# The head of an FFT filter and snake MLP kernel: PSUM as one block with rings, fewer and larger blocks of classes, products per filter part

## The chip, the cores and the metric

The kernel runs on one core of one Trainium2 chip. Its engines are TensorE (PE, with weight loads as PEld), VectorE (DVE), ScalarE (ACT), GpSimd (POOL) and SyncE (SP, which issues DMAs). Each engine works through its own queue in order and waits on semaphores for the others. The time is device microseconds of one execution.

## The reference

x has 8 batches of 3008 rows and 256 channels. Each batch is filtered in the frequency domain along its rows, and the 24,064 rows that result go through a two-layer network with the snake function.

```python
X = np.fft.rfft(x, axis=1)
Y = X * (filt_r + 1j * filt_i)[None]
x = np.fft.irfft(Y, n=3008, axis=1).reshape(24064, 256)
h = x @ w_in                                   # 256 -> 2048
g = h + np.sin(alpha * h) ** 2 / (alpha + 1e-9)
return g @ w_out                               # 2048 -> 256
```

## The kernel before, in words

**The transform.** 3008 is 47 x 64. A batch goes through a first small DFT over 47 (matmuls "pa"), a second one over 64 for each of 24 classes of frequencies ("pb", evicted as xf), products with the filter, the inverse of the second ("pc", evicted as g) and the inverse of the first ("pd", evicted as y). The filter lies in filt_t as two parts: f_t[0] holds filt_r and f_t[1] filt_i with signs, each on 128 partitions of which one half is loaded and the other is made on the chip by `other_half` (lines 439 to 446): a copy of 64x3072 elements for part 0, a negated one for part 1, each for two groups of 12 classes.

**The head** (lines 448 to 586) does batch 0 by itself, since nothing else can run yet. Turns of 32x32 blocks on VectorE (`turn`, line 473) take the place of trips through memory: four before the forward step, two large ones (`turn_back`) behind the inverse one. In between stand 12 blocks of 4 classes and 128 columns each (`blocks`, line 484). For each, `forward_0` has 4 matmuls and an eviction by ScalarE (line 495), `product_0` one VectorE product of 1024 elements that reads the block twice by a broadcast, once for each filter part (line 501), and `inverse_0` 8 matmuls (line 513) and an eviction, by ScalarE for all blocks (lines 516, 185). The loop of line 554 issues product i, inverse i-1, forward i+6, and in steps 5 and 6 the two halves of the filter's second group. `inverse_table` (line 420) makes a second table from the first through PSUM. `warm_pe` runs matmuls on zeros whose result nobody reads. Behind the last product GpSimd scales the weights w_in (line 542) and loads x of batch 1 in between (line 168).

**The main loop** (lines 746 to 760) has 48 chunks of rows. Eight steps a chunk each do two `hidden` (two ph matmuls, line 601; the sine on ScalarE as cos_all, line 605; v on VectorE, line 606) and some `project` (po matmuls, line 621, evicted as o at line 630 and stored). The transforms of batches 1 to 7 are placed into the steps by times written out by hand (`put` and `slot`): `first` and `first_tiled` (pa), `forward` (pb, xf), `product` and `cross` (the fused product of later batches), `inverse` (pc) and `last` (pd). `forward` evicts xf on ScalarE and sends its halves crosswise to xs by two DMAs on SP (line 250); `product` (line 257) reads xf, `cross` (lines 263, 264) reads xs.

**What sets the order around the change.** PSUM's eight banks are three pools: fps with two banks for all transform matmuls, hps with four for ph, warm-ups and the head's forward blocks, ops with two for po, the tables and the reciprocals. The SBUF pools xfpool (3 buffers), xspool (3) and ppool (7) hold xf, xs and the products. Whoever takes a buffer waits for the readers of its last tenant. Evictions by `evac` (line 182) without a given engine go to VectorE every third time and otherwise to ScalarE.

Of the kernel before, what the change touches and what calls it, by code (L numbers as in the profile page):

```python
# [9 lines left out]
FP16 = mybir.dt.float16  # L10
# [12 lines left out]
NR = 2 * N1  # L23
# [48 lines left out]
def kernel(  # L72
# [38 lines left out]
    xfpool = pool("xf", 3)  # L111
    ppool = pool("pp", 7)
    xspool = pool("xs", 3)
# [4 lines left out]
    fps = pool("fps", 2, PSUM)  # L118
    hps = pool("hps", 4, PSUM)
    ops = pool("ops", 2, PSUM)  # L120
# [31 lines left out]
    f_t = [filt_t[:, k] for k in range(2)]  # L152

# [35 lines left out]
    class Spectral:  # L189
# [13 lines left out]
        def first(self, i):  # L203
            ch, j = divmod(i, 4)
            ps = fps.tile([128, 512], FP32, name=f"pa_{self.b}_{i}", tag="f")
            marks["pe"] = nc.tensor.matmul(out=ps[0:NK, :], lhsT=wf_t, rhs=self.x[ch][:, 2 * j:2 * j + 2, :],  # L206
                                           start=True, stop=True)
            r0 = 8 * (ch % 2)
            evac(t1_h[ch // 2][0:NK, r0 + 2 * j:r0 + 2 * j + 2, :], ps[0:NK, :])
            if j == 3:  # L210
                nc.sync.dma_start(out=self.d1_rows[:, 8 * ch:8 * ch + 8, :], 
                                  in_=t1_h[ch // 2][0:NK, r0:r0 + 8, :])

        def first_tiled(self, ch):
            r0 = 8 * (ch % 2)
            for q in range(2):
                own, tag = (hps, "h") if q else (fps, "f")
                ps = [own.tile([128, 512], FP32, name=f"pa_{self.b}_{ch}_{q}_{h}", tag=tag) for h in range(2)]
                for h in range(2):
                    for c in range(2):  # L220
                        n = 4 * c + 2 * q
                        nc.tensor.matmul(out=ps[h][64 * c:64 * c + 64, :], lhsT=wt_t[64 * h:64 * h + N1],  # L222
                                         rhs=self.x[ch][64 * h:64 * h + N1, n:n + 2, :], start=True, stop=True)
                for h in range(2):
                    evac(t1_h[ch // 2][:, r0 + 4 * h + 2 * q:r0 + 4 * h + 2 * q + 2, :], ps[h], h == 0)
            d1 = self.d1.rearrange("a (h n) c -> a h (n c)", h=2)
            for c in range(2):
                n0 = (8 * ch + 4 * c) * C
                nc.sync.dma_start(out=d1[:, :, n0:n0 + 4 * C],
                                  in_=t1_h[ch // 2][64 * c:64 * c + 2 * NS, r0:r0 + 8, :]  # L230
                                  .rearrange("a (h n) c -> a h (n c)", h=2))
# [6 lines left out]
        def forward(self, u):  # L238
            b = self.b
            ps = fps.tile([128, 2, C], FP32, name=f"pb_{b}_{u}", tag="f")  # L240
            for i in range(2):
                s = 2 * u + i
                nc.tensor.matmul(out=ps[:, i, :], lhsT=d_t[:, s, :],  # L243
                                 rhs=self.t2[s // 6][:, s % 6, :], start=True, stop=True)
            self.xf[u] = xfpool.tile([128, 2, C], FP16, name=f"xf_{b}_{u}", tag="xf")
            nc.scalar.copy(out=self.xf[u], in_=ps)  # L246
            if self.fused:
                self.xs[u] = xspool.tile([128, 2, C], FP16, name=f"xs_{b}_{u}", tag="xs")
                for p in range(2):
                    nc.sync.dma_start(out=self.xs[u][64 * p:64 * p + 64, :, :],  # L250
                                      in_=self.xf[u][64 - 64 * p:128 - 64 * p, :, :])

        def product(self, u):
            self.p[u] = []
            for k in range(1 if self.fused else 2):
                pt = ppool.tile([128, 2, C], FP16, name=f"p_{self.b}_{u}_{k}", tag="p")
                marks["prod", u] = nc.vector.tensor_tensor(out=pt, in0=self.xf[u],  # L257
                                                           in1=f_t[k][:, 2 * u:2 * u + 2, :], op=ALU.mult)
                self.p[u].append(pt)
# [6 lines left out]
        def inverse(self, w):  # L266
# [4 lines left out]
            ps = fps.tile([128, 2, C], FP32, name=f"pc_{b}_{w}", tag="f")  # L271
# [12 lines left out]
        def inverse_tiled(self, w):  # L284
            g = gpool.tile([128, 4, 2, C], FP16, name=f"gt_{self.b}_{w}", tag="g")
            for q in range(2):
                own, tag = (hps, "h") if q else (fps, "f")
                ps = [own.tile([128, 2, C], FP32, name=f"pc_{self.b}_{w}_{q}_{k}", tag=tag) for k in range(2)]
# [20 lines left out]
        def last(self, u):  # L309
            ch, rest = divmod(u, 4)  # L310
            half, cb = divmod(rest, 2)
            n0 = 8 * ch + 4 * half
            ps = fps.tile([128, 4, 128], FP32, name=f"pd_{self.b}_{u}", tag="f")
            psv = ps.rearrange("p a b -> p (a b)")[:, 0:4 * NR].rearrange("p (a r) -> p a r", r=NR)
            for i in range(4):
                nc.tensor.matmul(out=psv[:, i, :], rhs=wi_t if self.b < TILED else wh_t, start=True, stop=True,  # L316
                                 lhsT=t4_h[ch // 2][0:NK, n0 % 16 + i, cb * 128:cb * 128 + 128])
            evac(y[:, cb, self.b % 2, n0:n0 + 4, :], psv)
# [29 lines left out]
    def spread_alpha(i):  # L348

        ps = hps.tile([128, 4, 128], FP32, name=f"al_bc_{i}", tag="h")  # L350
# [42 lines left out]
    def last_0(n0, n, own=fps, tag="f", spread=False):  # L393

        for cb in range(2):
            made = []

            def one(i, cb=cb, made=made):

                if i == 0:  # L400
                    ps = own.tile([128, 512], FP32, name=f"pd_0_{n0}_{cb}", tag=tag)
                    made.append(ps[:, 0:n * NR].rearrange("p (a r) -> p a r", r=NR))
# [11 lines left out]
    def reciprocals():  # L414

        ps = ops.tile([128, 512], FP32, name="ps_rec", tag="o")
# [3 lines left out]
    def inverse_table(g):  # L420

        gs = slice(8 * g, 8 * g + 8)
        ps = ops.tile([128, 8, 128], FP16, name=f"pse_{g}", tag="o")
# [6 lines left out]
    warmed = []  # L430

    def warm_pe(n):

        warmed.append(n)
        ps = hps.tile([128, 512], FP32, name=f"warm_{len(warmed)}", tag="h")
# [3 lines left out]
    def other_half(g, k, on_act):  # L439

        gs = slice(12 * g, 12 * g + 12)
        if k == 0:
            evac(f_t[0][64:128, gs, :], f_t[0][0:64, gs, :], on_act)
# [12 lines left out]
    for i in range(16):  # L456
        own, tag = (fps, "f") if i % 3 == 2 else (hps, "h")
        ps = own.tile([128, 512], FP32, name=f"pa_0_{i}", tag=tag)
# [21 lines left out]
    for i in range(4):  # L480
        turn(t2_0[i // 2][:, :, 32 * (i % 2):32 * (i % 2) + 32], t1_0[:, :, 32 * i:32 * i + 32])
        if i > 1:
            other_half(0, i - 2, False)
    blocks = [(hc, w) for hc in range(2) for w in range(3)] + [(0, 3), (1, 3), (0, 4), (0, 5), (1, 4), (1, 5)]
    xf0, p0 = {}, {}

    def forward_0(i):
        hc, w = blocks[i]
        ps = hps.tile([128, 4, 128], FP32, name=f"pb_0_{i}", tag="h")
        for j in range(4):  # L490
            nc.tensor.matmul(out=ps[:, j, :], lhsT=d_t[:, 4 * w + j, :],  # L491
                             rhs=t2_0[hc][:, 4 * w + j], start=True, stop=True)
        own, tag = (xspool, "xs") if i % 2 else (xfpool, "xf")
        xf0[i] = own.tile([128, 4, 128], FP16, name=f"xf_0_{i}", tag=tag)
# [3 lines left out]
    def product_0(i):  # L498
        hc, w = blocks[i]
        p0[i] = xpool.tile([128, 2, 4, 128], FP16, name=f"p_0_{i}", tag="x")  # L500
        marks["products"] = nc.vector.tensor_tensor(
            out=p0[i].rearrange("p f s (k c) -> p f s k c", k=2),
            in0=xf0[i].rearrange("p s (k c) -> p s k c", k=2)[:, None].to_broadcast([128, 2, 4, 2, 64]),
            in1=filt_t[:, :, 4 * w:4 * w + 4].rearrange("p f s (k c) -> p f s k c", k=2)[..., 64 * hc:64 * hc + 64],
            op=ALU.mult)

    def inverse_0(i):
        hc, w = blocks[i]
        ps = fps.tile([128, 4, 128], FP32, name=f"pc_0_{i}", tag="f")
        for j in range(4):  # L510
            s = 4 * w + j
            for k in range(2):
                nc.tensor.matmul(out=ps[:, j, :], rhs=p0[i][:, k, j, :],  # L513
                                 lhsT=e_t[:, s, :] if k == 0 else e1_0[:, s, :],
                                 start=(k == 0), stop=(k == 1))
        evac(g_0[hc][:, 4 * w:4 * w + 4], ps.rearrange("p s (k c) -> p s c k", k=2), not (i in ()))
# [31 lines left out]
    [inverse_table(g) for g in range(2)]  # L548
    for i in range(6):
        forward_0(i)  # L550
        if i % 3 == 2:
            if i == 2: inverse_table(2)
            warm_pe((4, 0)[i // 3])
    for i in range(13):
        for e in {5: [(1,0,False)],6: [(1,1,False)]}.get(i, ()):
            other_half(*e)
        if i < 12:
            product_0(i)
        if i == 11:
            reciprocals()  # L560
        if i > 0:
            inverse_0(i - 1)
        if i + 6 < 12:
            forward_0(i + 6)
        if i == 12:
            turn_back(0)
# [16 lines left out]
    warm_pe(12)  # L583
    last_0(0, 4)
    last_0(4, 2, hps, "h")
# [8 lines left out]
    def hidden(k, jb):  # L594
# [4 lines left out]
        ps = hps.tile([128, 512], FP32, name=f"ph_{k}_{jb}", tag="h")  # L599
# [10 lines left out]
    def project(k, u):  # L610
# [7 lines left out]
        if (t % 2 == 0 or alone) and half == 0:  # L618
            pso[k] = ops.tile([128, 2, C], FP32, name=f"po_{k}_{t}", tag="o")
# [79 lines left out]
    for n0, n, at in ((6, 5, 1.5), (11, 4, 11), (15, 4, 13), (19, 4, 15.5), (23, 4, 17), (27, 5, 19)):  # L699
        put(at, last_0, n0, n, fps, "f", True)  # L700
# [91 lines left out]
```

## Time and profile before

| | us |
|---|---|
| median of 3 runs | 777.34 (776.98 to 777.93) |
| the profiled execution | 779.76 |
| its span on the core | 778.0 |
| granted TensorE clock in it | 0.997 |
| first pd of the head; first ph | 36.98; 38.5 |

In the profile's lists an entry in order of time begins with start and duration in us from the span's start; "x5" counts instructions merged into one entry, and "[0.42 <-ACT t_h L185]" is idle time of the engine before it and what ended it. "t<-pa 128x512 f16<-128x512 f32" names what is written and read, with partitions x elements. A list of waits gives the waiting engine, its tile and line, whom it waited for, and then the total in us, how often, and the longest. The chain of waits is the page's part that follows the last instruction back to what released it.

### The profile page before, as it was taken

Reading aid. Unit: us, or ns where it says so; the run is one execution under the profiler, and the core shown is the slowest. Engines: PE = TensorE matmul, PEld = TensorE weight load, DVE = VectorE, ACT = ScalarE, POOL = GpSimd, SP = SyncE. Lnnn points to the kernel's source line nnn. Section 1 sums busy time; section 2 is a strip of 40 time slices with the busy share of each in tenths; the row PEclk is TensorE's granted clock in tenths of the full one; section 3 lists DMA queues with packets and bytes.
Section 4 is the critical chain, followed back from the end, with each engine's and each line's share of the span. In section 5 each row is a group of like instructions: output and inputs, shape, how many; then the busy total and the mean of one; then the engine's idle time right before and its main releaser. Section 6 shows DMA issues by size and latency. Waiting matters only on the chain.

```text
span 778.0 us, 17230 instructions
## 1 busy us (share of the span) xinstructions
PE 764.5 (98%) x6039; PEld 517.0 (66%) x6039; DVE 658.0 (85%) x1174; ACT 610.4 (78%) x1204; POOL 370.4 (48%) x649
## 2 busy tenths in 40 slices
PE   7999999999999999999999999999999999999997
PEld 3757766666666666666666666766666666766665
DVE  6986998999988888898889988898888888787773
ACT  5798888898878877888878787788778787777762
POOL 6355555634555655455464647554454645430000
PEclk9999999999999999999999999999999999999999
DMA  9955578864765428644474536864254322511112
GB/s 223 267 108 160 119 181 242 220 137 124 187 165 133 124 58 219 154 108 127 107 194 121 139 95 145 198 152 120 72 145 110 87 70 56 135 46 34 37 41 56
DMA packets 81518, 101.49 MB, mean 130 GB/s; under 512 B 18884, under 2 KB 60864, under 8 KB 81431
## 3 DMA queue, kind: packets, MB, share of 16 engines
q0 software_dynamic: 27440, 47.29, 26.1%
q1 hardware_dynamic: 53434, 52.79, 25.4%
q8 instruction: 47, 0.77, 0.4%
q10 hardware_dynamic: 557, 0.31, 0.2%
q14 instruction: 40, 0.33, 0.1%
HBM read 56.15 MB, written 46.66 MB: 132 GB/s over the span
## 4 chain that ended last, share of the span: by engine, by line
PE 91%; DVE 5%; ACT 1%; issue 1%; DMA 1%; ACTq 0%; DVEq 0%
PE po L621 40%; PE ph L601 40%; DVE v L606 3%; PE pd L316 2%; PE pb L243 2%; PE pa L222 2%; PE pc L293 1%; ACT cos_all L605 1%; PE pc L513 1%; DMA w<-in_moe_alpha_dram 1%; PE warm L437 1%; PE pb L491 1%; PE pa L459 1%; PE pa L206 0%; PE pd L403 0%
## 5 line engine op out<-in xcount | busy, mean ns | idle before, releaser
L606 DVE SCALAR_TENSOR_TENSOR v<-cos_all,ph 128x512 f16<-128x512 f32 (+1 forms) x768 | 482.5, 671 | 99.2 <-ACT cos_all L605 95.7
L605 ACT ACTIVATE cos_all<-ph 128x512 f32<-128x512 f32 (+1 forms) x768 | 413.9, 600 | 101.8 <-PE ph L601 98.5
L665 POOL DMA_DIRECT2D out_dram<-o x530 | 291.7, 557 | 244.1 <-ACT o L630 215.3
L621 PE MATMUL po<-w,v 128*128 128x256 f16 x3008 | 389.9, 273 | 0.9 <-DVE v L606 0.9
L601 PE MATMUL ph<-y,w 128*128 128x512 f16 (+1 forms) x1536 | 389.1, 375 | 1.3 <-DVE v L606 1.1
L621 PEld LDWEIGHTS <-v 128*128 128x128 f16 x3008 | 289.9, 98 | 85.9 <-DVE v L606 1.5
L601 PEld LDWEIGHTS <-w 128*128 128x128 f16 x1536 | 143.1, 98 | 114.0 <-issue 19.1
L630 ACT COPY o<-po 128x512 f32<-128x512 f32 (+1 forms) x95 | 56.1, 591 | 7.6 <-PE po L621 6.9
L246 ACT CAST xf<-pb 128x512 f16<-128x512 f32 x84 | 51.1, 608 | 2.0 <-PE pb L243 1.2
L185 ACT CAST y<-pd 128x376 f16<-128x376 f32 (+1 forms) x86 | 42.1, 491 | 12.3 <-PE pd L316 8.8
L160 POOL DMA_DIRECT2D x<-in_x_dram x48 | 25.6, 538 | 40.1 <-DVE v L606 26.8
L185 ACT CAST t_h<-pa 128x512 f16<-128x512 f32 (+1 forms) x60 | 32.8, 590 | 12.5 <-PE pa L222 11.3
L316 PEld LDWEIGHTS <-t_a 96*128 96x128 f16 x448 | 31.4, 97 | 12.7
L264 DVE TENSOR_TENSOR p<-p,xs 128x512 f16<-128x512 f16 x84 | 35.7, 425 | 2.9
L263 DVE TENSOR_TENSOR xs<-xs,filt_t 128x512 f16<-128x512 f16 x84 | 35.1, 418 | 1.6 <-DMA xs<-xf 1.6
L257 DVE TENSOR_TENSOR p<-xf,filt_t 128x512 f16<-128x512 f16 x84 | 35.0, 417 | 0.0
L185 ACT CAST gt<-pc 128x512 f16<-128x512 f32 x54 | 28.1, 595 | 8.4 <-PE pc L293 8.4
L187 DVE CAST t_h<-pa 128x512 f16<-128x512 f32 (+1 forms) x52 | 33.5, 682 | 0.2
L243 PE MATMUL pb<-t,d_t 128*128 128x256 f16 x168 | 32.1, 273 | 0.6 <-ACT cos_all L605 0.6
L316 PE MATMUL pd<-wh_t,t_a 96*128 96x94 f16 x384 | 31.8, 204 | 0.0
L235 POOL DMA_DIRECT2D t<-d x28 | 24.4, 874 | 12.0 <-DMA d<-t_h 10.9
L243 PEld LDWEIGHTS <-d_t 128*128 128x128 f16 x168 | 16.3, 98 | 15.1 <-DMA t<-d 0.8
(70 smaller groups left out, 278.0 us busy)
## 6 DMA issues: line engine op xcount, KB each, us to landing
t<-d POOLq DMA_DIRECT2D x28, 384.0 KB, 5.2
xs<-xf SPq DMA_DIRECT2D x168, 64.0 KB
t_a<-d SPq DMA_DIRECT2D x28, 384.0 KB
x<-in_x_dram POOLq DMA_DIRECT2D x50, 188.0 KB, 4.5
d<-t_h SPq DMA_DIRECT2D x48, 192.0 KB
d<-gt SPq DMA_DIRECT2D x36, 256.0 KB
out_dram<-o POOLq DMA_DIRECT2D x91, 64.0 KB, 2.1
out_dram<-o POOLq DMA_DIRECT2D x31, 80.0 KB, 3.6
```

Of the source, the lines that this page charges most:

```text
L185: marks["act"] = nc.scalar.copy(out=dst, in_=src)
L243: nc.tensor.matmul(out=ps[:, i, :], lhsT=d_t[:, s, :], rhs=self.t2[s // 6][:, s % 6, :], start=True, stop=True)
L246: nc.scalar.copy(out=self.xf[u], in_=ps)
L263: nc.vector.tensor_tensor(out=xs, in0=xs, in1=f_t[1][:, 2 * u:2 * u + 2, :], op=ALU.mult)
L264: nc.vector.tensor_tensor(out=p, in0=p, in1=xs, op=ALU.add)
L316: nc.tensor.matmul(out=psv[:, i, :], rhs=wi_t if self.b < TILED else wh_t, start=True, stop=True, lhsT=t4_h[ch // 2][0:NK, n0 % 16 + i, cb ...
L601: nc.tensor.matmul(out=ps[:, 0:n], lhsT=w1[:, cb, jb * 128:jb * 128 + 128], rhs=y_cols[:, cb, c0:c0 + n], start=(cb == 0), stop=(cb == 1))
L605: nc.scalar.activation(out=cs[:, 0:n], in_=ps[:, 0:n], func=AFT.Sin, bias=float(np.pi / 2))
L606: marks["snake"] = nc.vector.scalar_tensor_tensor(out=v[k][:, jb, 0:n], in0=cs[:, 0:n], scalar=-1.0, in1=ps[:, 0:n], op0=ALU.add, op1=ALU. ...
L621: nc.tensor.matmul(out=pso[k][:, t % 2, :], lhsT=v[k][:, jb, 128 * t:128 * t + 128], rhs=w2[:, jb, :], start=(jb == 0), stop=(jb == 15))
L630: copy(out=o[:, i0:t % 2 + 1, :], in_=pso[k][:, i0:t % 2 + 1, :])
L665: queues[i % len(queues)].dma_start(out=bass.AP(tensor=out.tensor, offset=out.offset + t0 * C, ap=[*ap, [1, C]]), in_=o_blk[p0:p0 + rows, :])
```

## The change

It does seven things:
- PSUM becomes one tile of eight banks. Three rings (`Ring`) deal its banks in strict rotation, 2, 4 and 2 of them, in place of the pools; a take of two banks gives neighbours.
- The head's 12 blocks of 4 classes become 8 blocks, of 8 and of 4 classes in turn (two groups, two column halves). A block of 8 is one pair of banks and one eviction of 1024 elements. Inverse blocks take fps for the even ones and ops for the odd ones, which are those with 4 classes.
- A product becomes two, one per filter part, with no broadcast operand.
- The first copy of `other_half` goes from VectorE to GpSimd (as 64x1536 words), behind GpSimd's loads of filter and table; the first negation and the second group's copy and negation stay on VectorE. All four first turns now stand ahead of the first negation; the second group's two are made ahead of product 4, the first block that needs them.
- The eviction of inverse block 4 goes to VectorE.
- Four forwards run ahead instead of six, the warm-up before the first pd has 8 matmuls instead of 12, and both large turns follow the loop.
- xf, xs and the products become pieces of one SBUF tile `work`: 2 pieces for xf (before 3 buffers), 4 for xs (before 3), 7 for products (before 7). The head's forward blocks use the same tile.

The diff, cut to its core (in the other places a tile of a pool becomes a `take()` of the ring of the same name):

```diff
-    fps = pool("fps", 2, PSUM)
-    hps = pool("hps", 4, PSUM)
-    ops = pool("ops", 2, PSUM)
+    psum = pool("psum", 1, PSUM).tile([128, 8, 512], FP32, name="psum")
+    class Ring:
+        def __init__(self, first, n):
+            self.first, self.n, self.at = first, n, 0
+        def take(self, n=1):
+            at = -(-self.at // n) * n % self.n
+            self.at = (at + n) % self.n
+            return psum[:, self.first + at:self.first + at + n].rearrange("p b c -> p (b c)")
+    fps, hps, ops = Ring(0, 2), Ring(2, 4), Ring(6, 2)
...
+    work = cpool.tile([128, 13, 512], FP16)
+    pieces = work.rearrange("p n (i c) -> p n i c", c=C)
...
-            self.xf[u] = xfpool.tile([128, 2, C], FP16, name=f"xf_{b}_{u}", tag="xf")
+            self.xf[u] = pieces[:, u % 2]
-                self.xs[u] = xspool.tile([128, 2, C], FP16, name=f"xs_{b}_{u}", tag="xs")
+                self.xs[u] = pieces[:, 2 + u % 4]
-                pt = ppool.tile([128, 2, C], FP16, name=f"p_{self.b}_{u}_{k}", tag="p")
+                pt = pieces[:, 6 + (12 * self.b + u) % 7]
...
+        if (g, k) == (0, 0):
+            nc.gpsimd.tensor_copy(out=f_t[0][64:128, gs].rearrange("p s c -> p (s c)").bitcast(UINT32),
+                                  in_=f_t[0][0:64, gs].rearrange("p s c -> p (s c)").bitcast(UINT32))
...
-    blocks = [(hc, w) for hc in range(2) for w in range(3)] + [(0, 3), (1, 3), (0, 4), (0, 5), (1, 4), (1, 5)]
+    blocks = [(hc, s0, n) for g in range(2) for hc in range(2) for s0, n in ((12 * g, 8), (12 * g + 8, 4))]
...
+        for f in range(2):
+            marks["products"] = nc.vector.tensor_tensor(
+                out=p0[i][:, f].rearrange("p s (k c) -> p s k c", k=2),
+                in0=xf0[i].rearrange("p s (k c) -> p s k c", k=2),
+                in1=f_t[f][:, s0:s0 + n].rearrange("p s (k c) -> p s k c", k=2)[..., 64 * hc:64 * hc + 64],
+                op=ALU.mult)
...
-        ps = fps.tile([128, 4, 128], FP32, name=f"pc_0_{i}", tag="f")
+        ps = (ops if i % 2 else fps).take(n // 4).rearrange("p (s c) -> p s c", c=128)
-        evac(g_0[hc][:, 4 * w:4 * w + 4], ps.rearrange("p s (k c) -> p s c k", k=2), not (i in ()))
+        evac(g_0[hc][:, s0:s0 + n], ps.rearrange("p s (k c) -> p s c k", k=2), i != 4)
...
+    for i in range(9):
+        if i == 4:
+            other_half(1, 0)
+            other_half(1, 1)
+        if i < 8:
+            product_0(i)
+        if i == 7:
+            reciprocals()
+        if i > 0:
+            inverse_0(i - 1)
+        if i + 4 < 8:
+            forward_0(i + 4)
+    turn_back(0)
     turn_back(1)
...
-    warm_pe(12)
+    warm_pe(8)
```

## The prediction

> **What bounds the kernel now.** I read the page first, then who waited for whom on TensorE, then the head (0 to 39 us) on each engine in order of time, then every wait of the two programs laid over the times of before.
>
> ```profile
> PE 764.5 (98%) x6039; PEld 517.0 (66%) x6039; DVE 658.0 (85%) x1174; ACT 610.4 (78%) x1204; POOL 370.4 (48%) x649
> ```
>
> The idle PE time lies nearly all in the head. From 39 us on, this is all that PE waited for (us in total, times, longest):
>
> ```profile
> PE ph L601 <- DVE v L606: 1.1, 4, 0.6
> PE po L621 <- DVE v L606: 0.9, 3, 0.3
> PE pb L243 <- ACT cos_all L605: 0.6, 1, 0.6
> PE pd L403 <- ACT xf L246: 0.4, 1, 0.4
> PE pa L206 <- ACT t_h L185: 0.4, 1, 0.4
> PE pa L206 <- ACT y L185: 0.2, 1, 0.2
> ```
>
> These 3.6 us are all that the main loop has to give; a new PE stall there goes whole into the time, for nothing behind it has slack. In the head VectorE is the bound: it works without a gap from 15.72 to 32.3.
>
> ```profile
> 18.02 1.20 DVE L473 STREAM_TRANSPOSE t<-t 128x1024 uint32<-128x1024 uint32 x1
> 19.23 0.95 DVE L187 COPY filt_t<-filt_t 64x3072 f16<-64x3072 f16 x1
> 20.20 1.25 DVE L473 STREAM_TRANSPOSE t<-t 128x1024 uint32<-128x1024 uint32 x1
> 21.48 0.96 DVE L445 TENSOR_SCALAR filt_t<-filt_t 64x3072 f16<-64x3072 f16 x1
> 22.54 3.10 DVE L501 TENSOR_TENSOR p<-xf,filt_t 128x1024 f16<-128x1024 f16 x5
> ...
> 28.47 3.70 DVE L501 TENSOR_TENSOR p<-xf,filt_t 128x1024 f16<-128x1024 f16 x6
> 32.09 0.17 DVE L418 TENSOR_SCALAR rec_t<-ps_rec 128x16 f32<-128x16 f32 x1
> 32.42 4.50 DVE L473 STREAM_TRANSPOSE t_a<-t_h 128x2048 uint32<-128x2048 uint32 x2 [0.16 <-ACT t_h L185]
> ```
>
> The two turns back end at 36.92; PE's pd starts at 36.98 and ph follows. So the head is worth what VectorE's row is worth.
>
> **The head, VectorE row by row.** The copy of 19.23 goes to GpSimd: -0.97 (start to start). Products: 12 of 1024 elements at 0.61 (five in 3.10, six in 3.70) become 8 of 1024 and 8 of 512. The row nearest to a 512 is L257, whose two in a row took 0.76 with 0.42 for one: 0.34 each. 8 x 0.61 + 8 x 0.34 - 12 x 0.61 = +0.3. Block 4's eviction moves from ScalarE to VectorE: L187 takes 512 elements from PSUM in 0.69, and 0.60 from start to start in the main loop, so 1024 cost about 1.14 (0.60 + 512 x 1.05 ns, the slope of L187 between 376 and 512 elements: 0.55 to 0.69). It also waits: VectorE is done with block 5's products 0.69 after block 4's, but TensorE needs 0.14 to start (the "issue" piece between a product and its pc), 16 matmuls at 0.056 and 0.17 until the last lands, 1.2 in all. So VectorE stands for 0.5. Against that the 0.16 wait at 32.42 falls away, and the changes between copies, transposes and products, which cost 0.1 to 0.3 extra each, become fewer (-0.2).
>
> -0.97 + 0.3 + 1.14 + 0.5 - 0.16 - 0.2 = **+0.6** on the end of the turns. Bounds: -0.5 if VectorE finds other waits hidden in this stand, +1.2 if neither of the last two credits comes. Had ScalarE kept block 4, it would be -1.0.
>
> What lies beside it: eight forward evictions instead of twelve on ScalarE (1024 by the L428 row 0.91 apart, two 512s 0.95) save 0.4 of an engine that is not late; forward 4 stands on TensorE until block 2 is evicted (about 22.9), while VectorE has products until 25.2. Warm-ups go from 12 to 8 and end 1 us before pd; the 0.97 idle at 28.3 was followed by matmuls at the old 0.056. GpSimd's weights start with the last product, 0.8 later (w2's third part then ends at 50.5, first used after 52).
>
> **The copy on GpSimd** has no row. It may start when the last DMA issue is out:
>
> ```profile
> 16.15 0.58 POOL L368 DMA_DIRECT2D e_t<-e_tbl  x1
> 32.26 4.84 POOL L542 TENSOR_TENSOR w<-w_in,y 128x768 f16<-128x768 f32 x3 [15.54 <-DVE rec_t L418]
> ```
>
> 1536 words at between 0.8 ns (its CAST of 16 against 128 elements, 0.19 to 0.28) and 2.4 ns (768 in 1.85) take 1.4 to 3.7: done at 18.2 to 20.5. The first product is due at 21.5, so I take nothing. The three L542 above ran beside VectorE's transposes in 4.84 against 5.02 for the same shapes at 37.63 to 43.6, so transposes do not hold it. [...]
>
> **PSUM as rings: the main loop.** The pools did not rotate strictly. They handed out the bank that came free first: at 50.06 pa 2 took the bank of pa 1, whose eviction by ScalarE ended at 50.01. The ring gives it the bank of pa 0, which VectorE evicts only now:
>
> ```profile
> 50.06 0.38 PE L206 MATMUL pa<-x,wf_t 94*96 94x512 f16 x1 [0.42 <-ACT t_h L185]
> 50.30 0.68 DVE L187 CAST t_h<-pa 96x512 f16<-96x512 f32 x1
> ```
>
> VectorE is late there because it works through 16 v in a row from 39.86 (0.60 each); the change doesn't touch that. PE waits to 50.98 + 0.1: +1.0. Laying every wait of the changed program over these times gives four more where TensorE would start before its bank is free: 56.59 (VectorE ends 56.73, +0.25), 63.65 (63.80, +0.25), 77.74 (ScalarE's y ends 78.14, +0.45) and 128.38 (VectorE 128.80, +0.5). ScalarE gets 79 more wait instructions, 0.04 each by their rows: 3 us of an engine 78% busy, nothing. Together **+2.5**; bounds 1.5 (hand-over free, and the two small ones lost) to 3.
>
> **xf with two buffers.** A forward eviction now waits for the products and sends of two forwards before, not three. From batch 3 on the slack is 6.9 us or more. In batch 2, forward 6 (ScalarE at 166.72) waits for product 4, which VectorE ends at 168.05; TensorE's pd of 168.17 needs the bank that this empties: **+0.6**. In batch 1 the sends land too late by 2.35, 2.40, 2.62 and 0.91 us (forwards 5, 8, 9, 10), as they went before. But those sends were themselves late, waiting for one of three xs buffers:
>
> ```profile
> SPq L250 <- DVE p L264: 10.3, 9, 3.1
> ```
>
> Four xs buffers let them go 1.2 to 1.7 earlier, two of them ahead of the loads of x (84.3, 92.5) behind which they queued. That leaves forward 9, about 1.2. TensorE can run two steps (3.9 us) on four ph banks, while a bank takes about 2.5 (0.4 ph, 0.6 cos, 0.7 v and the queues), so a ScalarE stall of 1.2 shows little: **+0.3**; bounds 0 and 3 (the four stalls whole, less 1.4 each, and the lag that stays on VectorE, 98% busy there).
>
> **The sum**: 0.6 + 2.5 + 0.6 + 0.3 = +4.0 on a span of 778.0, in an execution of 779.76. The unprofiled runs have a median of 777.34, 2.4 below that execution; I add the difference to the median: **781.3**.
>
> **Rivals.** A measurement tells about 0.2% (1.55 us) from no change: below 775.8 is faster, above 778.9 slower.
> - The ring waits are not there (other lags on VectorE at the five points): 777.34 + 1.5 = 778.8. Against it: the lag at 50 comes from work that stays. 12%.
> - Not slower by cheaper products: if plain operands ran at the copy row's 0.31 ns an element (0.95 for 3072) instead of 0.52, the 12,288 elements save 2.6, head -2.0, in all +1.4: 778.7. It decides from 0.41 or less for 1024. Against it: L257 has plain operands already and pays 0.34 for 512. 6%.
> - The sends in batch 1 are no earlier: 781.3 + 2.7 = 784.0. For it: they share the queues with loads and stores. 12%.
> - The copy is held until the transposes end (20.4), and ends at 22 to 24: products wait 0.4 to 2.6, +1.5: 782.8. Against it: the L542 row. 5%.
> - Something in the head that I don't see (the two-part products letting TensorE start earlier, ScalarE being what paces), with the ring harmless: about 775. 10%.
>
> The forecast itself, 779.9 to 782.9, has 55%. Faster 0.10, same 0.18, slower 0.72. The range 778.0 to 784.0 takes in all but the last rival and part of the third.
>
> **What would show it.** Right: VectorE's turns back end at about 37.5; a VectorE eviction of 128x1024 near 29.8 with 0.5 idle before it; PE idle 1.0 near 50.7 "<-DVE"; a new "ACT xf <-DVE p" wait near 170; PE's waits after the head near 7 us in all, not 3.6. Wrong: turns back ending before 36.5, products of 512 under 0.3, or PE's waits after the head unchanged.

## The result and the profile after

| | before | after |
|---|---|---|
| median, us | 777.6 (776.98 to 778.56, 6 runs) | 782.56 (781.77 to 783.75, 6 runs) |
| ratio to before | 1 | 1.0064 (1.0046 to 1.0082) |
| profiled execution; its span | 779.76; 778.0 | 781.77; 779.9 |
| start of the first turn | 15.72 | 13.83 |
| first turn to first pd | 21.26 | 22.23 |
| first pd to the end of the span | 741.0 | 743.9 |

The change costs 5.0 us (0.0064 x 777.6). The two profiled executions are only 2.0 apart, because that of before was one of its long ones: 3.4 us at half the granted clock lay in its first stage (mean granted clock 0.79 from 8 to 16 us, against 1.00 in the changed kernel). So I compare by stages from the first turn on: +0.97 in the head, +2.9 behind it. (The expectations below write 743.8 for the 743.9, from a span rounded to 0.1.)

The page's first line of the changed kernel, and all of TensorE's waits from 39 us on (us in total, times, longest):

```profile
PE 763.1 (98%) x6035; PEld 516.5 (66%) x6035; DVE 659.1 (85%) x1178; ACT 609.4 (78%) x1195; POOL 372.9 (48%) x650
```

```profile
PE psum L605 <- DVE v L610: 1.5, 5, 0.6
PE psum L215 <- DVE t_h L196: 1.4, 1, 1.4
PE psum L408 <- ACT y L194: 0.9, 1, 0.9
PE psum L625 <- DVE v L610: 0.6, 2, 0.3
PE psum L322 <- ACT work L254: 0.4, 1, 0.4
PE psum L322 <- DVE y L196: 0.4, 1, 0.4
PE psum L251 <- ACT work L254: 0.2, 1, 0.2
PE psum L215 <- DVE y L196: 0.2, 1, 0.2
```

The busy shares tell nothing apart; the waits do: 5.6 us where there were 3.6. L215 is pa, L408 and L322 are pd, L251 is pb; "<- ACT work" is a bank emptied late because ScalarE had no free piece for xf. All of these tiles bear one name now (psum, work), so the line has to tell which is meant. The longest of the waits stands at the place that the prediction names:

```profile
50.12 0.38 PE L215 MATMUL psum<-x,wf_t 94*96 94x512 f16 x1 [1.40 <-DVE t_h L196]
```

VectorE in the head of the changed kernel, in order of time:

```profile
18.48 0.96 DVE L450 TENSOR_SCALAR filt_t<-filt_t 64x3072 f16<-64x3072 f16 x1
19.47 3.84 DVE L504 TENSOR_TENSOR p<-work,filt_t 128x1024 f16<-128x1024 f16 x8
23.34 0.95 DVE L448 COPY filt_t<-filt_t 64x3072 f16<-64x3072 f16 x1
24.33 0.96 DVE L450 TENSOR_SCALAR filt_t<-filt_t 64x3072 f16<-64x3072 f16 x1
25.32 1.97 DVE L504 TENSOR_TENSOR p<-work,filt_t 128x1024 f16<-128x1024 f16 x4
28.41 1.23 DVE L196 CAST t_h<-psum 128x1024 f16<-128x1024 f32 x1 [1.13 <-PE psum L515]
29.55 1.96 DVE L504 TENSOR_TENSOR p<-work,filt_t 128x1024 f16<-128x1024 f16 x4
31.42 0.17 DVE L423 TENSOR_SCALAR rec_t<-psum 128x16 f32<-128x16 f32 x1
31.50 4.50 DVE L477 STREAM_TRANSPOSE t_a<-t_h 128x2048 uint32<-128x2048 uint32 x2
```

The copy is gone from the row, and in its place stand block 4's eviction, 1.14 from start to start, and 1.13 of waiting ahead of it. What that wait is shows on the other two engines: ScalarE is busy without a gap (22.36 to 28.18), and TensorE's inverse of block 4 can't start before ScalarE has emptied block 2's pair of banks.

```profile
25.18 1.04 ACT L497 CAST work<-psum 128x1024 f16<-128x1024 f32 x1
26.08 1.12 ACT L194 CAST t_h<-psum 128x1024 f16<-128x1024 f32 x1
27.03 0.65 ACT L497 CAST work<-psum 128x512 f16<-128x512 f32 x1
```

```profile
27.25 0.22 PE L515 MATMUL psum<-p,e_t 128*128 128x128 f16 x1 [0.48 <-ACT t_h L194]
```

ScalarE in the main loop of the changed kernel, at the two places where xf waits for one of its two pieces:

```profile
99.74 0.59 ACT L254 CAST work<-psum 128x512 f16<-128x512 f32 x1 [1.86 <-DMA work<-work]
...
169.46 0.59 ACT L254 CAST work<-psum 128x512 f16<-128x512 f32 x1 [1.24 <-PE psum L322]
```

At 99.74 the sender of the piece's last tenant had not landed. At 169.46 the profile names the matmul, which was long done; what ended then was VectorE's product 4 (168.96 to 169.38), the last reader of the piece.

### The profile page after: what moved, and what is told of

Read it like the earlier page. It is cut to its first block, busy times and chain, and to the rows that moved or that the text cites. A ratio compares the mean times of both kernels' runs of the same rounds, so it can differ in the third digit from the quotient of the medians.

```text
span 779.9 us, 17272 instructions
## 1 busy us (share of the span) xinstructions
PE 763.1 (98%) x6035; PEld 516.5 (66%) x6035; DVE 659.1 (85%) x1178; ACT 609.4 (78%) x1195; POOL 372.9 (48%) x650
## 4 chain that ended last, share of the span: by engine, by line
PE 81%; DVE 7%; DMA 6%; ACT 3%; issue 2%; POOL 1%; ACTq 0%; SPq 0%; DVEq 0%; POOLq 0%
PE psum L625 37%; PE psum L605 37%; DVE v L610 5%; PE psum L322 2%; PE psum L251 2%; ACT cos_all L609 2%; PE psum L230 1%; DMA d_t<-d_tbl 1%; DMA out_dram<-o 1%; PE psum L300 1%; DMA w_out<-in_moe_w_out_dram 1%; DMA w_in<-in_moe_w_in_dram 1%; DMA filt_t<-in_filt_r_dram 1%; POOL out_dram L669 1%; DVE work L272 0%
## 5 line engine op out<-in xcount | busy, mean ns | idle before, releaser
L610 DVE SCALAR_TENSOR_TENSOR v<-cos_all,psum 128x512 f16<-128x512 f32 (+1 forms) x768 | 483.0, 672 | 100.7 <-ACT cos_all L609 96.9
L609 ACT ACTIVATE cos_all<-psum 128x512 f32<-128x512 f32 (+1 forms) x768 | 414.1, 600 | 102.0 <-PE psum L605 98.3
L605 PE MATMUL psum<-y,w 128*128 128x512 f16 (+1 forms) x1536 | 389.3, 375 | 1.6 <-DVE v L610 1.5
L625 PE MATMUL psum<-w,v 128*128 128x256 f16 x3008 | 389.9, 273 | 0.6 <-DVE v L610 0.6
L605 PEld LDWEIGHTS <-w 128*128 128x128 f16 x1536 | 143.2, 98 | 115.0 <-issue 20.2
L634 ACT COPY o<-psum 128x512 f32<-128x512 f32 (+1 forms) x95 | 56.2, 592 | 7.6 <-PE psum L625 6.8
L254 ACT CAST work<-psum 128x512 f16<-128x512 f32 x84 | 50.9, 606 | 4.3 <-DMA work<-work 1.9
L194 ACT CAST y<-psum 128x376 f16<-128x376 f32 (+1 forms) x86 | 41.8, 488 | 11.9 <-PE psum L322 8.7
L194 ACT CAST t_h<-psum 128x512 f16<-128x512 f32 (+2 forms) x67 | 38.5, 616 | 15.7 <-PE psum L230 10.7
L322 PEld LDWEIGHTS <-t_a 96*128 96x128 f16 x448 | 31.4, 97 | 13.7 <-issue 1.2
L272 DVE TENSOR_TENSOR work<-work 128x512 f16<-128x512 f16 x84 | 35.7, 425 | 2.9
L271 DVE TENSOR_TENSOR work<-work,filt_t 128x512 f16<-128x512 f16 x84 | 35.3, 420 | 1.2 <-DMA work<-work 1.0
L265 DVE TENSOR_TENSOR work<-work,filt_t 128x512 f16<-128x512 f16 x84 | 35.1, 419 | 0.6 <-ACT work L254 0.6
L251 PE MATMUL psum<-t,d_t 128*128 128x256 f16 x168 | 32.1, 273 | 0.2 <-ACT work L254 0.2
L322 PE MATMUL psum<-wh_t,t_a 96*128 96x94 f16 x384 | 31.8, 204 | 0.0
L251 PEld LDWEIGHTS <-d_t 128*128 128x128 f16 x168 | 16.3, 98 | 14.7 <-issue 0.5
```

The costliest lines, as they stand in the source:

```text
L194: marks["act"] = nc.scalar.copy(out=dst, in_=src)
L251: nc.tensor.matmul(out=ps[:, i, :], lhsT=d_t[:, s, :], rhs=self.t2[s // 6][:, s % 6, :], start=True, stop=True)
L271: nc.vector.tensor_tensor(out=xs, in0=xs, in1=f_t[1][:, 2 * u:2 * u + 2, :], op=ALU.mult)
L272: nc.vector.tensor_tensor(out=p, in0=p, in1=xs, op=ALU.add)
L605: nc.tensor.matmul(out=ps[:, 0:n], lhsT=w1[:, cb, jb * 128:jb * 128 + 128], rhs=y_cols[:, cb, c0:c0 + n], start=(cb == 0), stop=(cb == 1))
L609: nc.scalar.activation(out=cs[:, 0:n], in_=ps[:, 0:n], func=AFT.Sin, bias=float(np.pi / 2))
```

## The experiments

All times of a row were taken beside runs of the kernel before on the same chip; the ratio is to those. The stage columns come from one profile each. To set two edits against each other I take the difference of their ratios times 777.6; by the two intervals (0.0018 for the changed kernel, 0.0010 to 0.0018 for the other) such a difference is uncertain by 1.6 to 2.0 us, so the places that gain are read from the profiles. Profiles with * have a stretch of 3.4 us at half the granted clock between 31 and 36 us, which lengthens the matmuls ahead of pd (24 of psum<-w,one take 2.19, 2.04 and 2.77 us in runs 1, 2 and 4, and 1.50 in the changed kernel).

| kernel | median, us | ratio to before | turn to pd | pd to end |
|---|---|---|---|---|
| changed kernel | 782.56 | 1.0064 (1.0046 to 1.0082) | 22.23 | 743.9 |
| with the pools' order (1) | 780.43 | 1.0029 (1.0018 to 1.0040) | 23.02* | 741.6 |
| with 3 xf, 3 xs (2) | 796.98 | 1.0241 (1.0221 to 1.0261) | 23.02* | 756.4 |
| with block 4 on ScalarE (3) | 780.48 | 1.0039 (1.0021 to 1.0056) | 21.13 | 743.8 |
| with the copy on VectorE (4) | 782.75 | 1.0059 (1.0043 to 1.0076) | 23.38* | 744.2 |
| with 3 xf, 6 products (5) | 779.83 | 1.0032 (1.0020 to 1.0045) | 22.43 | 742.0 |
| with 1, 3 and 5 (6) | 775.87 | 0.9980 (0.9970 to 0.9989) | 20.70 | 739.7 |
| before, copy on GpSimd (7) | 778.09 | 1.0012 (1.0002 to 1.0022) | 20.94 | 742.5 |
| before, again (8) | 778.75, one run | | 21.26 | 741.9 |
| before, with rings (9) | 779.84 | 1.0029 (1.0018 to 1.0040) | 21.26 | 743.5 |
| 6 with the copy on VectorE (10) | 776.48 | 0.9985 (0.9977 to 0.9994) | 21.02 | 740.0 |
| 6 with one product a block (11) | 776.00 | 0.9990 (0.9972 to 1.0009) | 20.68 | 739.8 |

**1. The pools' order, played back in the ring.** The seven places where the pools had given the bank of the take before once more:

```diff
-        def take(self, n=1):
+        def take(self, n=1, again=False):
+            if again:
+                self.at = (self.at - n) % self.n
...
-            ps = fps.take()
+            ps = fps.take(again=self.b == 1 and i in (2, 8, 15))
...
-            ps = fps.take().rearrange("p (i c) -> p i c", c=C)
+            ps = fps.take(again=(b, u) == (1, 3)).rearrange("p (i c) -> p i c", c=C)
...
-            psv = fps.take()[:, 0:4 * NR].rearrange("p (a r) -> p a r", r=NR)
+            psv = fps.take(again=(self.b, u) == (1, 2))[:, 0:4 * NR].rearrange("p (a r) -> p a r", r=NR)
...
-                    made.append(own.take()[:, 0:n * NR].rearrange("p (a r) -> p a r", r=NR))
+                    made.append(own.take(again=n0 == 27)[:, 0:n * NR].rearrange("p (a r) -> p a r", r=NR))
```

> The changed kernel, in which seven takes of the two-bank ring (first of batch 1 at i = 2, 8 and 15, last_0 of positions 27 to 31 in both column blocks, forward 3 and last 2 of batch 1) get the bank of the take before again, as the pools of the kernel before had dealt them. Theory (the strict order costs the waits of TensorE at 50.1, 56.7, 77.8 and 128 us): the matmuls behind the head end 2.0 to 2.5 us earlier, less what the order gave back at 73.4 us (0.77 us), so the stretch from the first last step to the end of the span goes from 743.8 to 741.4 to 742.6; TensorE's wait for L196's tile t_h at 50.1 (1.40 us) and for y at 77.8 (0.89 us) are gone. Rival (these waits only show what TensorE would lose elsewhere, because VectorE and ScalarE bound that stretch): the waits move, and the stretch stays at 743.8 within 0.3.

Behind the head it is 743.9 to 741.6, and 2.7 us by the runs. TensorE's longest waits in this kernel from 39 us on:

```profile
PE psum L607 <- DVE v L612: 1.5, 5, 0.6
PE psum L627 <- DVE v L612: 0.6, 2, 0.3
PE psum L410 <- ACT work L256: 0.4, 1, 0.4
PE psum L217 <- ACT t_h L196: 0.4, 1, 0.4
PE psum L324 <- ACT work L256: 0.4, 1, 0.4
...
```

The 1.4 of pa for VectorE is 0.4 for ScalarE again, as before; the 0.9 of pd for y is gone. The theory holds: the waits do not move elsewhere. Laid against the profile of before from the end, matmul by matmul, the changed kernel loses 1.0 at 50, 0.35 at 57 and 64 together, 0.44 at 78 and 0.49 at 128 us, 2.3 in all, and this kernel loses none of these.

**2. Three pieces for xf, three for xs.**

```diff
-            self.xf[u] = pieces[:, u % 2]
+            self.xf[u] = pieces[:, u % 3]
-                self.xs[u] = pieces[:, 2 + u % 4]
+                self.xs[u] = pieces[:, 3 + u % 3]
```

> The changed kernel with three pieces in turn for xf instead of two, and three for xs instead of four. Theory (two xf pieces make ScalarE wait for the swap's transfers at 99.7 us and for product 4 at 169.5 us, and TensorE behind it): the stretch from the first last step to the end goes down by 1.0 to 1.6 us from 743.8; ScalarE's waits of 1.86 and 1.24 us are gone, and TensorE's of 0.43 near 170 and of 0.23 near 103. Rival (the three xs pieces in turn hold SP back instead, and the transfers come later): SP waits for VectorE as it did before (10 us in sum), and the stretch stays at 743.8 within 0.3.

This changed the computation: in batch 1 the transfers of forward u+3 stand ahead of the cross product of u in the program, and with three pieces of a tile the product of u then reads slot u+3's transfer, and waits for it. VectorE's waits of this kind, from 39 us on, are 1.0 us in the changed kernel and here:

```profile
DVE work L271 <- DMA work<-work: 15.2, 10, 4.8
```

So it says nothing of xf. It does say why the change has four pieces for xs: in the kernel before, with its pool of three buffers, the fourth transfer waited for the first buffer's readers, though they come later in the program (SyncE's waits of 10.3 us), while with three places in a tile it was the reader that waited for the transfer (the 15.2 us here).

**3. Block 4's eviction on ScalarE**: `i != 4` becomes `True`.

> The changed kernel with the eviction of block 4's inverse on ScalarE, like the other seven. Theory (VectorE bounds the head; that eviction, 1.23 us with its stand of 1.13, is 2.36 us of its queue, of which 1.0 goes into waiting for ScalarE's evictions of blocks 4 and 5 ahead of the first turn back): first turn to first last step goes from 22.2 to 20.7 to 21.0 us, the rest stays at 743.8, the time 1.2 to 1.6 us lower. By the prediction's sum it would be 1.6. Rival (ScalarE is as full as VectorE there, so the turns back only wait for it): less than 0.5 us.

The runs say 1.9 us, which is just the size of their uncertainty; the profile says 1.1 in the head (22.23 to 21.13). VectorE in this kernel:

```profile
19.25 1.18 DVE L450 TENSOR_SCALAR filt_t<-filt_t 64x3072 f16<-64x3072 f16 x1 [0.72 <-DMA filt_t<-in_filt_i_dram]
20.46 3.84 DVE L504 TENSOR_TENSOR p<-work,filt_t 128x1024 f16<-128x1024 f16 x8
...
26.30 3.84 DVE L504 TENSOR_TENSOR p<-work,filt_t 128x1024 f16<-128x1024 f16 x8
30.06 0.17 DVE L423 TENSOR_SCALAR rec_t<-psum 128x16 f32<-128x16 f32 x1
30.43 4.54 DVE L477 STREAM_TRANSPOSE t_a<-t_h 128x2048 uint32<-128x2048 uint32 x2 [0.21 <-ACT t_h L194]
```

From the first product to the turns back it is 9.97 (20.46 to 30.43) against 12.03: 2.06 gained, of which this execution lost 0.94 ahead of the products to a filter that landed late (0.72) and a negation that took longer (0.22, see 6). Of the 2.36 that the eviction put into VectorE's row, ScalarE takes back only 0.21 at the end: the rival is out. The 2.06 is not all to be had, though, for a VectorE that comes to the turns earlier waits longer there: in run 6, where the filter was in time, it waits 0.37, and the turns end 20.64 after the first one's start instead of 22.17, 1.5 less.

**4. The copy on VectorE**, at the place where the changed kernel issues it to GpSimd.

> The changed kernel with the copy of the filter's first half on VectorE, as before the change. Theory 1 (VectorE bounds the head from the first turn on, all that is put on it counts): first turn to first last step goes from 22.2 to 23.2 us (+0.97). Theory 2 (the stand of 1.13 us ahead of block 4's eviction waits for ScalarE and takes up the delay of VectorE): +0.0 to +0.5, and the stand shrinks by as much as the copy puts in.

Theory 2. The changed kernel and this one can't be told apart (1.0064 and 1.0059), and the wait ahead of block 4's eviction shrinks from 1.13 to 0.49:

```profile
26.03 1.97 DVE L503 TENSOR_TENSOR p<-work,filt_t 128x1024 f16<-128x1024 f16 x4
28.49 1.23 DVE L196 CAST t_h<-psum 128x1024 f16<-128x1024 f32 x1 [0.49 <-PE psum L514]
...
31.58 4.50 DVE L476 STREAM_TRANSPOSE t_a<-t_h 128x2048 uint32<-128x2048 uint32 x2
```

By the end of the turns, which the slow clock of this profile does not touch (they take 4.50 here as in the changed kernel), it is 22.52 from the first turn against 22.17: 0.35 of the copy's 0.97 arrive. The rest is waited for anyway.

**5. Three pieces for xf, six for the products**, the four of xs kept:

```diff
-            self.xf[u] = pieces[:, u % 2]
+            self.xf[u] = pieces[:, u % 3]
-                self.xs[u] = pieces[:, 2 + u % 4]
+                self.xs[u] = pieces[:, 3 + u % 4]
-                pt = pieces[:, 6 + (12 * self.b + u) % 7]
+                pt = pieces[:, 7 + (12 * self.b + u) % 6]
```

> The changed kernel with xf in three pieces in turn instead of two, xs in four as changed, and the products in six instead of seven. (In the run with three pieces for xs, a transfer wrote a piece of xs before the cross product that reads it had come, so it computed with another slot's data and waited for its transfer: its 14 us are the price of that order and say nothing of xf.) Theory (two xf pieces cost ScalarE's waits at 99.7 and 169.5 us, and TensorE behind it): the stretch from the first last step to the end of the span goes from 743.8 to 742.2 to 742.9, the time down by 0.9 to 1.6 us; ScalarE's waits of 1.86 for the swap's transfer and 1.24 us for product 4 are gone, and TensorE's of 0.43 near 170 and 0.23 near 103. Rival (six product pieces hold VectorE back instead, the inverse being late): VectorE waits for TensorE at a product, and the time stays within 0.4 us of the changed kernel's.

743.9 to 742.0 behind the head, and 2.5 us by the runs, a little more than expected. The eviction that stood at 169.46 in the changed kernel follows without a wait:

```profile
165.84 1.13 ACT L609 ACTIVATE cos_all<-psum 128x512 f32<-128x512 f32 x2
166.81 0.65 ACT L254 CAST work<-psum 128x512 f16<-128x512 f32 x1
```

Against the changed kernel, matmul by matmul and by that kernel's times, TensorE gains 0.13 at 102, 0.39 at 103, 0.23 by 116, 0.62 at 170 and 0.55 by 174 us, 1.9 in all. The last is an echo: ph waited for VectorE's v, which the stall of cos had made late; in the list of waits, L605's for v go from 1.5 us in five to 1.1 in four. The rival is out, VectorE never waits for a product piece.

**6. All three edits.**

> The three edits together: the pools' order of the two-bank ring, three pieces for xf with six for the products, block 4's eviction on ScalarE. Theory (three causes at three places, which add): 2.1 + 1.2 + 2.0 us less than the changed kernel by the runs so far, so 777.2 to 777.6 against a median of 782.6, and 1.0 us below the kernel before, which is what the head's copy on GpSimd and the missing wait are worth. Rival (what one edit brings is given back at the same next wait, the filter's landing in the head or SP's transfers): 778.5 or more, no faster than the kernel before.

6.5 us less than the changed kernel by the ratios, where the three alone make 2.7 + 1.9 + 2.5 = 7.1: they add, within what the runs can tell; 6.5 is more than the 5.3 expected. By the profiles the two edits behind the head add closely: 2.3 and 1.9 apart, 4.2 together (743.9 to 739.7). It is the fastest of the study, 0.2% below the kernel before, and its matmuls show that nothing of the change's loss is left: from the first pd to 73 us they run at the times of before, there the wait of 0.6 for a transfer is missing (0.8 gained, see 8), and from then on they keep that lead. GpSimd's copy in it, and what VectorE does beside it and at the end of the head:

```profile
16.92 1.46 POOL L447 COPY filt_t<-filt_t 64x1536 uint32<-64x1536 uint32 x1
```

```profile
17.97 1.23 DVE L452 TENSOR_SCALAR filt_t<-filt_t 64x3072 f16<-64x3072 f16 x1
...
28.83 0.17 DVE L425 TENSOR_SCALAR rec_t<-psum 128x16 f32<-128x16 f32 x1
29.36 4.55 DVE L479 STREAM_TRANSPOSE t_a<-t_h 128x2048 uint32<-128x2048 uint32 x2 [0.37 <-ACT t_h L196]
```

The negation takes 1.23 where it takes 0.96 in the changed kernel, and the turns back wait 0.37 for ScalarE. So of what the copy saves, part is lost beside it and part ends in a new wait. Runs 10, 11 and 7 size this.

**7. The kernel before with the copy on GpSimd alone.**

> The kernel before with one edit: the first copy of the filter (64x3072 fp16, 0.95 us on VectorE) as uint32 on GpSimd. Theory (VectorE bounds the head, so what leaves its queue goes into the time, less what VectorE loses beside GpSimd's 1.46 us): 0.6 to 1.0 us faster than the kernel before, with the turns back ending 20.2 to 20.6 us after the first turn's start instead of 21.2. Rival (VectorE then waits for the filter's landing, for GpSimd's copy or for the evictions of ScalarE): 0 to 0.3 us.

In the head it is the rival: the turns back start 16.38 after the first turn (13.15 to 29.53) where before they start at 16.70: 0.32 of 0.97. VectorE now waits for things that it had covered:

```profile
18.04 1.05 DVE L448 TENSOR_SCALAR filt_t<-filt_t 64x3072 f16<-64x3072 f16 x1 [0.27 <-DMA filt_t<-in_filt_i_dram]
19.27 3.10 DVE L504 TENSOR_TENSOR p<-xf,filt_t 128x1024 f16<-128x1024 f16 x5 [0.19 <-DVE filt_t L448]
...
29.06 0.17 DVE L418 TENSOR_SCALAR rec_t<-ps_rec 128x16 f32<-128x16 f32 x1 [0.15 <-PE ps_rec L417]
29.53 4.50 DVE L476 STREAM_TRANSPOSE t_a<-t_h 128x2048 uint32<-128x2048 uint32 x2 [0.30 <-ACT t_h L185]
```

And the time is 0.9 us longer (0.0012 x 777.7, interval 0.2 to 1.7), which neither theory had. Behind the head, the pools dealt other banks at two places and TensorE waits 0.2 (pa for y) and 0.4 (pd for t_h) more at 61 and 62 us; laid over the first profile of before this costs 0.9, and 0.8 come back near 71 us, where the transfer is in time. What else is lost stands at 143 us (0.7, a load of x that the second profile of before waits for too, see 8) and in small steps between 183 and 440 us (0.9). These I can't put down to the copy, so the 0.9 of the runs stays unexplained.

**8. The kernel before, a second profile.**

> The kernel before, unchanged, for a second profile of it. Theory (the profile of before was of one of its longer executions: a stretch of 3.4 us at half the granted clock lay in its first stage, and TensorE waited 0.6 us at 73.4 us for a transfer that another execution would have in time): the span is 775 to 776.5, the first turn starts at 13 to 14 us and not 15.7, and no wait of TensorE stands near 73 us. Rival (both belong to the kernel before): first turn at 15.5 or later, with the wait of 0.6 us near 73.

Half of each: the first turn starts at 13.87, as in the changed kernel, and the head is 21.26 again. Most of the 1.9 us between the two starts fits the clock: 3.41 us at half of it cost at most 1.7. The span of 777.0 is above the 776.5 expected. But the wait near 73 us belongs to the kernel:

```profile
71.78 0.39 PE L243 MATMUL pb<-t,d_t 128*128 128x256 f16 x2 [0.82 <-DMA t<-d]
```

Its part behind the head took 741.9, 0.9 more than in the first profile; half of that is a wait of 0.5 for a load of x. This is the size of difference that one profile can't tell.

**9. The rings in the kernel before**, nothing else: each pool tile of PSUM becomes a `take()`.

> The kernel before with one edit: PSUM as one tile dealt in strict turn from rings of 2, 4 and 2 banks; head, products, copies and xf, xs and p pools as before. Theory (the strict order alone costs TensorE 2.3 us behind the head: 1.0 at 50, 0.2 and 0.15 near 57 and 64, 0.44 at 78, 0.49 at 128): 1.5 to 2.3 us slower than the kernel before, the lower end where a later TensorE has no more to wait for the transfer near 72 us (0.6 to 0.8 us before). Rival (the order costs only together with the changed head or the two pieces for xf): within 0.4 us of the kernel before.

2.3 us slower by the runs (0.0029 x 777.7, interval 1.4 to 3.1), and TensorE's waits for its banks are those of the changed kernel:

```profile
PE psum L216 <- DVE t_h L197: 1.4, 1, 1.4
PE psum L413 <- ACT y L195: 0.9, 1, 0.9
...
PE psum L326 <- DVE y L197: 0.4, 1, 0.4
PE psum L216 <- DVE y L197: 0.2, 1, 0.2
```

The head is 21.26, as before, and matmul by matmul the five places cost 2.2. So the strict order costs this by itself, and the rival is out; it is the largest single part of the loss, shown from both sides (1 and 9). But the 2.5 that the profile loses behind the head (741.0 to 743.5) are not these five places alone: the wait near 73 us is gone (0.8 gained), and at 344 us VectorE waited for a crosswise transfer, which cost TensorE 1.3 and stands in no profile of the kernel before:

```profile
343.97 0.42 DVE L273 TENSOR_TENSOR xs<-xs,filt_t 128x512 f16<-128x512 f16 x1 [2.33 <-DMA xs<-xf]
```

Whether that late transfer belongs to the rings is not shown. The size rests on run 1, where neither of the two differs: 2.3.

**10 and 11. The fastest version with the copy back on VectorE, and with one product for each block.**

> The three edits together, with the first copy of the filter back on VectorE. Theory (VectorE's queue bounds the head, but it loses about 0.27 us to the GpSimd copy beside it, in the TENSOR_SCALAR that took 1.23 us instead of 0.96, and waits 0.37 us for ScalarE ahead of the turns back): 0.97 - 0.27 - 0.37, so 0.3 to 0.5 us slower than the three edits alone. Rival 1 (the whole copy counts): 0.9 to 1.0 us slower. Rival 2 (VectorE beside GpSimd loses what the copy saves, as the kernel before with this copy alone came out no faster): 0 or faster.

> The three edits together, with one product instruction for each block, its first operand broadcast over the two filter parts, as in the kernel before. Theory (an instruction less for each block saves VectorE 8 x 0.04 = 0.3 us by the rows of both kernels, but VectorE already waits 0.37 us for ScalarE at the end of the head): within 0.2 us of the three edits alone. Rival 1 (VectorE's queue still bounds): 0.3 us faster. Rival 2 (the broadcast form costs more at 2048 elements): slower by over 0.3 us.

The copy on GpSimd is worth 0.32 in the head (21.02 against 20.70), as the theory says; the runs (0.4 by the ratios, intervals overlapping) do not speak against it. The one product leaves the head where it was (20.68 against 20.70), as the theory says; by the ratios it is 0.8 us slower, but its interval takes in the other's. It saves VectorE 0.28 on four blocks and hands it to ScalarE:

```profile
24.91 3.56 DVE L505 TENSOR_TENSOR p<-work,filt_t 128x2048 f16<-128x2048 f16 x4
28.39 0.17 DVE L425 TENSOR_SCALAR rec_t<-psum 128x16 f32<-128x16 f32 x1
29.23 4.54 DVE L479 STREAM_TRANSPOSE t_a<-t_h 128x2048 uint32<-128x2048 uint32 x2 [0.67 <-ACT t_h L196]
```

3.56 instead of 3.84, and a wait of 0.67 instead of 0.37. So once block 4 is ScalarE's again, it is ScalarE that the turns back wait for.

## Why the prediction was right, and where its terms were off

The time came 1.3 us above the forecast and inside its range; the case was the forecast's own. The causes were named rightly, but that their sum came so close is in part luck: the head and xf cost 1.4 more than forecast, the rings 0.2 less, and a gain of 0.8 and some 0.5 at the program's end were not foreseen. By its steps:

- **The rings, +2.5.** Right in kind, in places and in size: 2.3 by the matmuls' times, and 2.7 by run 1 (run 9's 2.3 is a sum in which other things count too). The stall at 50 is 1.40 in all, 1.0 of it new. All five points were found by laying the waits of the new order over the old times. The first rival, 778.8, fell here.
- **The head, +0.6.** It is +0.97. The failing step is "So VectorE stands for 0.5": it stood 1.13, because I called ScalarE "an engine that is not late". It works without a gap from 22.36 to 28.2, and the inverse of block 4 needs a whole pair of banks that ScalarE empties only at 27.2. The other rows came out as sized: eviction 1.14 as taken, products +0.28 for +0.3, the copy's 0.97 off VectorE's row. The changes between instructions gave back 0.45, not 0.2. The line "Had ScalarE kept block 4, it would be -1.0" was near: with run 6's edits the head is 20.70, 0.56 below before, in an execution where the negation beside the copy took 0.27 longer.
- **The copy on GpSimd, taken at nothing.** Hidden as said (17.11 to 18.57, the first product at 19.47). But its credit of 0.97 was not to be had: 0.35 in run 4, 0.32 in runs 7 and 10. The row lost 0.97, the end of the row did not, for other waits stood behind it. In the changed kernel this and the stand of 1.13 are one thing: with the copy on VectorE, the stand is 0.49.
- **xf with two pieces, +0.6 and +0.3.** The two stalls are there, at forward 9 of batch 1 and forward 6 of batch 2 (99.74 and 169.46), but they cost 1.9 by the trace and 2.5 by the runs. Mis-sized: batch 1's 0.3 is 0.75 (0.13, 0.39 and 0.23), and behind batch 2's 0.62 comes another 0.55. I counted a stall of ScalarE to the first matmul that it held and not to the next v, which the late cos delays in turn. The rival of the sends being no earlier, 784.0, is out: of its four waits only one showed.
- **The other rivals.** Plain operands are not cheaper (four products of 1024 and four of 512 in 3.84), and the copy is not held by the transposes: it ran beside them in 1.46. The last rival, 775, had in "ScalarE being what paces" what made VectorE stand, but it expected this to make the time shorter.
- **Not foreseen:** TensorE's wait for t2 near 73 us (0.60 and 0.82 in the two profiles of before) is gone in the changed kernel, a gain of 0.8. The store of t_h and the load behind it took 4.96 us from the last eviction's end to the load's issue before (64.65 to 69.61) and 3.58 after (65.05 to 68.63). It took near 3.6 in runs 1, 6, 7 and 9 too, so it goes neither with the order of the banks nor with the head's blocks; what shortens it was not tried and stays open.
- **The signs.** The stall near 50, the wait of xf near 170 and an idle VectorE ahead of block 4's eviction are there. Two signs did not come as written. The turns back end at 36.0, which by the letter is the sign of "wrong" (before 36.5), because this execution's first turn started 1.9 earlier; from the first turn on it is 22.17, where the forecast's 37.5 means 21.8. And TensorE's waits come to 5.6 and not 7; 0.6 of the difference is the wait near 73 that is gone.

The sum by the trace is +0.97 + 2.3 + 1.9 - 0.8, less 0.5 in the last matmuls and stores: +3.9 from the first turn to the end, against +4.0 forecast. (Against the second profile of before, run 8, it is 3.0.) The runs say 5.0, with an interval of 3.6 to 6.4. The missing 1.1 is no part of the change that I can name: 0.8 of it is that the profiled execution of after was the shortest of its six, that much below their median.

## What to carry to other kernels

Two buffers dealt in strict turn, whose readers are two engines of different lag, made TensorE wait for the later one at five places here; handing out what is free first had avoided that. So before a pool is replaced by a ring, lay the new waits over the old times. Taking work off an engine that "bounds" a stage is worth only the distance to the next wait in its row (0.3 of 0.97 here): read ScalarE's and TensorE's rows beside VectorE's before a row is counted as time. A stall that an engine passes on can come back one step later through the buffers that it refills (0.55 behind 0.62 here), so size it to where the rows meet again, not to the first matmul.

## What the runs showed of the hardware that was not expected

GpSimd's plain copy of 64x1536 words took 1.46 us in the profiles of the changed kernel and of runs 3, 5, 6, 7 and 11, 0.95 ns a word. VectorE's negation of 64x3072 fp16 (0.96 us alone, at 21.48 in the kernel before) stretched when it started while the copy ran: by 0.01, 0.09, 0.21, 0.22 and 0.27 us where 0.16, 0.23, 0.36, 0.37 and 0.41 us of the copy were left (runs 11, 7, 5, 3, 6). That is the time left less about 0.14, as if it stood still until the copy was done; the copy took no longer. What makes it wait is not shown, and the prediction's sum has no term for it.

A stretch at half the granted clock lay in the first 40 us of four of these thirteen profiles (before, runs 1, 2 and 4) and in none of the others', early in one and late in three. In that of before the granted clock is 0.50 from 8.70 to 12.11 us, 3.41 us in all, and 1.00 on both sides. In run 1 it is 0.95 in the mean from 24 to 32 us and 0.84 from 32 to 40, in run 2 0.99 and 0.80, in run 4 0.57 from 31.5 to 35.5: at half, that comes to 3.4 us in each. What starts it is not shown. What it costs depends on where it falls: up to 1.7 us ahead of the first turn (an estimate, half of the 3.41), and in run 4, in front of pd, 0.8 (0.86 us from the end of the turns to pd, against 0.06 in the changed kernel).
